# The order of the first loads in a gated linear attention and mixture-of-experts kernel

## The chip, the cores and the metric

One NeuronCore of a Trainium2 chip runs the whole program. The metric is device time in microseconds of one execution. The kernel before takes 376.09 us (median of three runs, 374.07 to 376.36).

## What is computed

The reference has two parts. The first is a gated linear attention: 4 batches, 8 heads, 768 positions, 48 channels a head. For every batch and head a 48 x 48 state is carried along the positions:

```
f = 1 / (1 + exp(-f_logit))
for t in range(S):
    state = f[:, :, t, :, None] * state + einsum('bhd,bhe->bhde', k[:, :, t], v[:, :, t])
    y[:, :, t] = einsum('bhd,bhde->bhe', q[:, :, t], state)
```

The second part takes the 3072 rows of 384 channels as tokens: `logits = x @ w_gate`, each token goes to its best of 8 experts, in order of arrival up to a capacity of 768, an expert is relu(x w1) w2 with 1024 hidden channels, and the row is scaled by its softmax weight.

## The kernel before

**Blocks and slots.** Attention runs over 24 blocks of 128 positions, six to a batch. The order of the work is written out by hand: `prologue()` brings the first blocks in, and `slot(n)` for n from 0 to 24 issues one stage of several blocks. In slot n, TensorE (PE) transposes k and q of block n+2 (`kq_in`), makes the scores of block n+1 (`scores_pe`), adds to block n what the state carries in (`inter`), updates the state (`update`), applies the masked scores of block n to v (`values`), and turns block n-1 into token rows with gate logits (`rows_pe`). Each engine runs its instructions in the order in which this code issues them, so an instruction that waits holds all that stands behind it on its engine.

**The other engines.** VectorE (DVE) makes the decays by scans (`decay`, `decay_back`) and scales the transposed k and q. ScalarE (ACT) takes the sigmoid of the gates of two blocks at a time (`sig`, tile pf) and copies PSUM out. GpSimd (POOL) copies k and q of a block into a padded tile (`kq_pad`, tile kqp), masks the scores (tile AT, L434), makes the carried state (`carry`, tile S, L508), and sends token rows to their expert's rows in DRAM by an indirect DMA (`scatter`, L326, tensor disp). The first of these scatters is issued in slot 7, one a slot after that.

**Loads.** SyncE (SP) issues nearly all loads. `load` fills the next of 3 tiles of gates (f, two blocks each), 3 of k and q (kq), or 6 of v. `late_constants` (L278) fetches the gate weights, four small transfers into the tile identc that `rows_pe` multiplies by; in the prologue they stand behind k, q of block 3 and v of block 1. `zero_disp` (L345) clears 256 rows of disp by one transfer of 402 KB from a tile of zeros: for expert 0 in the list of loads of slot 1, for the ninth group of rows in that of slot 3. A scatter writes the same tensor, so the first of them waits until the clears have landed.

**PE's fillers.** In the prologue `keep_busy` puts 7, 4 and 2 multiplications of the identity between the first steps. Transposing k and q of one block is one loop in which an instruction on partitions 0 to 63 (k) is followed by one on 64 to 127 (q).

Of the kernel before, what the change touches and what calls it, by code (L numbers as in the profile page):

```python
# [9 lines left out]
F32 = mybir.dt.float32  # L10
# [4 lines left out]
AF = mybir.ActivationFunctionType  # L15
# [5 lines left out]
P = 128  # L21
# [8 lines left out]
def kernel(  # L30
# [12 lines left out]
    nc = tc.nc  # L43
    B, H, S, D = q.shape
    N, DM = out.shape
    NE = w_gate.shape[1]
    DF = w1.shape[2]
    NP = H // 2
    HALF = 384
    C = 128  # L50
# [32 lines left out]
    psT = ctx.enter_context(tc.tile_pool(name="psT", bufs=2, space=PSUM))  # L83
# [96 lines left out]
    loads, pf, kqp = {}, [], []  # L180
    for nm in ("f", "kq", "v"):
        for i in range(NLOAD[nm]):
            if nm == "v":
                t = apool.tile([P, H, 64], F32, name=f"ld_{nm}{i}")
                nc.gpsimd.memset(t[:, :, D:], 0.0)
            else:
                t = apool.tile([P, H, 2, D], F32, name=f"ld_{nm}{i}")
            loads[nm, i] = t
    for made, nm, n in ((pf, "pf", 2), (kqp, "kqp", 2)):
        for i in range(n):  # L190
            t = apool.tile([P, 2, H, 64], F32, name=f"{nm}{i}")
# [3 lines left out]
    def pairs(nm, n, nt):  # L195
        b, t0 = n // CPB, n % CPB * C
        return srcs[nm][b, :, t0 : t0 + nt, :].rearrange("h (t j) d -> t h (j d)", j=2)

    def load(nm, n):
        if n >= (NT // 2 if nm == "f" else NT):  # L200
            return
        t = loads[nm, n % NLOAD[nm]]
        if nm == "v":
            b, t0 = n // CPB, n % CPB * C
            nc.sync.dma_start(t[:, :, :D], srcs[nm][b, :, t0 : t0 + C, :].rearrange("h p d -> p h d"))
            return
        t = t.rearrange("t h j d -> t h (j d)")
        if nm == "kq":
            for h, x in enumerate(nm):
                nc.sync.dma_start(t[64 * h : 64 * h + 64], pairs(x, n, C))  # L210
        elif n == 0:
            for h, queue in enumerate((nc.sync, nc.scalar)):
                hs = slice(4 * h, 4 * h + 4)
                queue.dma_start(t[:64, hs], pairs(nm, 0, C)[:, hs])
        else:
            nc.sync.dma_start(t, pairs(nm, 2 * n, 2 * C))

    def loaded(nm, n):
        return loads[nm, n % NLOAD[nm]]

    for nm, n in (("f", 0), ("kq", 0), ("kq", 1), ("f", 1), ("kq", 2), ("v", 0), ("f", 2)):
        load(nm, n)
        if (nm, n) == ("kq", 0):
            nc.sync.dma_start(loads["f", 0].rearrange("t h j d -> t h (j d)")[64:], pairs("f", 1, C))
# [5 lines left out]
    for i in range(2):  # L230
        t = apool.tile([P, NP * C], F32, name=f"Suf{i}")
# [5 lines left out]
    for i in range(2):  # L237
        t = apool.tile([P, NP, 64], F32, name=f"S{i}")
# [12 lines left out]
    identc = const.tile([P, NP, XW], F32, name="identc")  # L251
    put_off(nc.gpsimd.memset, identc, 0.0)
    for g in range(2):
        r = slice(64 * g, 64 * g + D)
        for b in range(2):
            h = g ^ b
# [21 lines left out]
    def late_constants():  # L278
        gates_of = w_gate.rearrange("(a b s d) e -> b s d a e", b=2, s=2, d=D)
        for g in range(2):  # L280
            for b in range(2):
                nc.sync.dma_start(identc[64 * g : 64 * g + D, b::2, 2 * D :], gates_of[b, g ^ b])
    ohc = const.tile([P, NE], BF16, name="ohc")
    lt = const.tile([P, NS, NS], F32, name="lt")
    put_off(nc.gpsimd.memset, lt, 1.0)
# [14 lines left out]
    for i in range(2):  # L300
        t = const.tile([P, NE], BF16, name=f"base{i}")
# [43 lines left out]
    def zero_disp(v):  # L345
        ins = nc.sync.dma_start(
            disp[v * RPE : v * RPE + 2 * P, :].rearrange("(a p) w -> p a w", p=P),
            zero.unsqueeze(1).broadcast_to([P, 2, W]),
        )
        after(ins, pace["ins"], "behind the first loads")  # L350

    def sig(u):
        if u >= NT // 2:
            return
        cuts = (0, 64, P) if u == 0 else (0, P)
        for r0, r1 in zip(cuts, cuts[1:]):
            pace["ins"] = nc.scalar.activation(
                pf[u % 2][r0:r1, :, :, :D], loaded("f", u)[r0:r1].rearrange("t h j d -> t j h d"), AF.Sigmoid
            ).ins

    def transposes(*dsts):
        for p in range(NP):
            for j in range(2):
                for t, src, h in dsts:
                    r = slice(64 * h, 64 * h + 64)
                    nc.tensor.transpose(  # L366
                        t[:R, p, j::2], src[r, j, 2 * p : 2 * p + 2].rearrange("t s d -> t (s d)")[:, :R], ident[r, r]
                    )
        return [t[:R].rearrange("r p t -> r (p t)") for t, src, h in dsts]
# [3 lines left out]
    def keep_busy(m):  # L373
        pw = psA.tile([P, P], F32, name="psA")
        for _ in range(m):
            nc.tensor.matmul(pw, ident, ident, start=True, stop=True)  # L376

    def f_in(*ns):
        made = [(psF.tile([P, NP, C], F32, name="psF"), pf[n // 2 % 2], n % 2) for n in ns]
        for n, F in zip(ns, transposes(*made)):  # L380
            Fs[n] = F
# [21 lines left out]
    def kq_pad(n):  # L403
        if n < NT:
            src = loaded("kq", n).rearrange("t h j d -> t j h d")
            if n - 3 < PAD_ACT:
                nc.gpsimd.tensor_copy(kqp[n % 2][:, :, :, :D], src)
            else:
                nc.scalar.activation(kqp[n % 2][:, :, :, :D], src, AF.Copy)

    def kq_in(n):
        pts = transposes(*((psT.tile([P, NP, C], F32, name="psT"), kqp[n % 2], h) for h in range(2)))
        for nm, pt, by, made in (("kT", pts[0], Sufb[n % 2], kTs), ("qT", pts[1], Rqs.pop(n), qTs)):
            t = abuf.tile([P, NP, C], F32, name=nm, bufs=3)
            nc.vector.tensor_tensor(t[:R].rearrange("r p t -> r (p t)"), pt, by[:R], op=ALU.mult)
            made[n] = t
# [120 lines left out]
    def rows_pe(n):  # L537
        yT = yTs.pop(n)
        px = psA.tile([P, NP, XW], F32, name="psA")
        for p in range(NP):  # L540
            for t in range(2):
                ts = slice(64 * t, 64 * t + 64)
                m_pe = nc.tensor.matmul(px[ts, p, :], yT[:R, p, ts], identc[:R, p, :], start=True, stop=True)  # L543
        marks[n] = [m_pe]
        return px
# [3 lines left out]
    def row_at(n):  # L549
        return ring[:, n % RING]  # L550
# [136 lines left out]
    def flush_scatter():  # L687
        if queue:
            n = queue.pop(0)
            late = n >= SPLIT  # L690
            ins = scatter(disp, ri_of.pop(n), row_at(n), NV * RPE - 1, ("disp", "late") if late else ("disp",))
            if not late:
                early_ins[:] = [ins]
# [76 lines left out]
    def prologue():  # L770
        keep_busy(7)
        nc.scalar.activation(warm, direv[:, :1], AF.Sigmoid)
        sig(0)
        f_in(0)
        decay_back(0, decay(0))
        kq_pad(0)
        load("kq", 3)
        load("v", 1)
        late_constants()
        keep_busy(4)  # L780
        kq_in(0)
        f_in(1)
        decay_back(1, decay(1))
        kq_pad(1)
        later_ops(put_off_ops)
        keep_busy(2)
        kq_in(1)
        sig(1)
        kq_pad(2)
        pas = scores_pe(0)  # L790
        f_in(2)
        decay_back(2, decay(2))
        scores_out(0, pas)
        pks = keys_pe(0)
        keys_out(0, pks)
        f_in(3)
        load("kq", 4)
        load("v", 2)
        load("kq", 5)
        load("f", 3)  # L800
    ends = {g + m - 1: (g, m) for g, m in GROUPS}

    def rank(g, pool):
# [8 lines left out]
    def loads_of(n):  # L812
        load("v", n + 3)
        if 0 < n < PAD_ACT:
            load("kq", n + 6)
        if n == 0:
            load("f", 4)
        if n == 2:
            nc.sync.dma_start(cap_i, capacity.bitcast(I32).partition_broadcast(P))
        if n in (1, 3):  # L820
            zero_disp(0 if n == 1 else NE)
        for k, at in enumerate(PIECE_LOAD):
            if at == n:
                pieces[k] = weight_piece(wsets[0], 0, raw0, k)

    def slot(n):
# [17 lines left out]
            choose_first(*half.pop())  # L844
        for g in full:
            choose_sum(*g)
        if n == 1:
            f_in(4)
        if kqn:
            kq_in(n + 2)  # L850
        if n % 2 and fn and n not in (1, 9, 15):
            f_in(n + 3, n + 4)
        if nxt:
            scores_out(n + 1, pas)
        if n == 0:
            sig(2)
        if prev and cur and first(n):
            y_out(n - 1)
# [31 lines left out]
        if nxt:  # L890
            for s in range(SCATTERS.get(n, 2)):
                flush_scatter()
        if fn:
            F = decay(n + 3)
        if prev:
            px = rows_pe(n - 1)
            if tail:
                rows_logits(n - 1, px)
                rows_copy(n - 1, px)
                chosen[n - 1] = choose_one(row_at(n - 1), abuf, tallies[-1][:, 1:2]), 1  # L900
            else:
                rows_copy(n - 1, px)
                rows_parts(n - 1, px)
# [15 lines left out]
        while full:  # L919
            g = full.pop()  # L920
            half.append((*g, choose_max(*g)))
        if prev and done and not tail:
            g, m = done
# [11 lines left out]
        if tail:  # L935
            early_job(n, 2)
            g, m = done
# [325 lines left out]
    xgs, made = {}, {}  # L1263
# [227 lines left out]
```

## Time and profile before

| what | before |
|---|---|
| median of three runs | 376.09 us |
| the profiled execution | 375.17 us, span 373.4 us, granted clock 0.99 |
| PE busy | 362.1 us, 97% of the span |
| DVE, ACT, POOL busy | 247.8, 223.8, 166.5 us |
| moved by DMA | 67.86 MB, mean 182 GB/s |

Attention fills the first 150 us or so of the span, the experts the rest. The page shows PE above nine tenths in nearly all of 40 slices, and the 16 DMA engines above nine tenths in the slices from 9 to 121 us.

### The profile page before, as it was taken

What the parts mean: (1) busy time and instruction counts of PE and PEld (TensorE: products, weight loads), DVE (VectorE), ACT (ScalarE), POOL (GpSimd) and SP (SyncE); (2) the same over time, 40 slices, a digit from 0 to 9 for tenths busy, and PEclk for the clock granted to TensorE, in tenths of its full rate; (3) what the DMA queues carried; (4) which work ended last, traced back from release to release, by engine and by line L of the source; (5) the groups of instructions that cost most, each with busy time, mean ns of one, the idle gap of its engine ahead of it and who ended that gap; (6) DMA issues with size and microseconds to landing.
All of it is one profiled execution on the core that took longest, in us unless ns stands there. A gap on an engine that the chain in (4) does not pass through costs nothing.

```text
span 373.4 us, 10082 instructions
## 1 busy us (share of the span) xinstructions
PE 362.1 (97%) x3895; PEld 340.8 (91%) x3895; DVE 247.8 (66%) x533; ACT 223.8 (60%) x458; POOL 166.5 (45%) x275
## 2 busy tenths in 40 slices
PE   8999999999899999999999999999999999999993
PEld 7999898888787889999899999999999999999993
DVE  4898988979687866753676296857757665570300
ACT  3356677877586763255477475759578586583310
POOL 6665556675757675235613702127117244144012
PEclk9999999999899999999999999999999999999997
DMA  8999999999997432476696979799797997721001
GB/s 153 187 177 224 205 207 227 256 214 226 213 227 164 130 114 105 133 237 204 191 239 188 286 196 242 212 187 319 169 204 247 172 208 253 129 94 52 14 23 40
DMA packets 111351, 67.86 MB, mean 182 GB/s; under 512 B 93646, under 2 KB 105844, under 8 KB 111296
## 3 DMA queue, kind: packets, MB, share of 16 engines
q1 hardware_dynamic: 107504, 57.09, 69.1%
q0 software_dynamic: 3520, 9.97, 7.7%
q8 instruction: 32, 0.52, 0.6%
q14 instruction: 23, 0.19, 0.2%
q10 hardware_dynamic: 272, 0.10, 0.1%
HBM read 49.46 MB, written 11.43 MB: 163 GB/s over the span
## 4 chain that ended last, share of the span: by engine, by line
PE 84%; issue 8%; ACT 3%; POOL 2%; DVE 1%; POOLq 1%; ACTq 0%
PE psM L1222 15%; PE psA L754 9%; PE psM L1015 9%; PE psT L754 9%; PE psM L754 7%; PE psA L426 6%; PE psY L522 6%; PE psA L543 5%; PE psT L366 4%; PE psY L468 3%; PE psA L488 3%; PE psT L451 3%; PE psF L366 2%; POOL out_dram L326 2%; PE psA L376 2%
## 5 line engine op out<-in xcount | busy, mean ns | idle before, releaser
L326 POOL DMA_INDIRECT out_dram<-yo,g_ti x30 | 31.3, 1042 | 55.6 <-ACT yo L1019 31.7
L434 POOL TENSOR_SCALAR_AFFINE_SELECT AT<-AT 128x512 f32<-128x512 f32 x48 | 29.4, 637 | 23.3 <-ACT AT L432 23.2
L1015 PE MATMUL psM<-w2h,hh 128*128 128x384 f32 (+2 forms) x112 | 37.5, 340 | 0.0
L1015 PE MATMUL psM<-w2l,hh 128*128 128x384 f32 (+2 forms) x112 | 37.3, 338 | 0.0
L1015 PE MATMUL psM<-w2h,hl 128*128 128x384 f32 (+2 forms) x112 | 37.2, 338 | 0.0
L135 ACT ACTIVATE w2h<-raw 128x768 fp32r<-128x768 f32 x32 | 27.0, 844 | 11.2 <-DMA raw<-in_moe_w_dram 11.2
L1222 PE MATMUL psM<-hh,w2h 128*128 128x440 f32 (+3 forms) x96 | 33.7, 351 | 0.0
L1222 PE MATMUL psM<-hh,w2l 128*128 128x440 f32 (+3 forms) x96 | 33.7, 351 | 0.0
L1222 PE MATMUL psM<-hl,w2h 128*128 128x440 f32 (+3 forms) x96 | 33.6, 350 | 0.0
L144 DVE TENSOR_TENSOR w2l<-raw,w2h 128x768 fp32r<-128x768 f32 x28 | 27.8, 994 | 7.7 <-ACT w2h L135 6.9
L386 DVE TENSOR_TENSOR_SCAN Suf<-psF,direv 112x511 f32<-112x511 f32 x24 | 29.1, 1212 | 4.5 <-PE psF L366 4.5
L432 ACT ACTIVATE AT<-psA 128x512 f32<-128x512 f32 x48 | 26.4, 612 | 8.9 <-PE psA L426 5.6
L1242 POOL COPY yo<-yq 128x384 uint16<-128x384 uint16 (+4 forms) x16 | 11.9, 790 | 40.1 <-DMA yq<-yp 38.2
L426 PE MATMUL psA<-qT,kT 48*128 48x128 f32 x384 | 29.4, 293 | 0.0
L400 DVE TENSOR_TENSOR_SCAN Rq<-psF,d 112x512 f32<-112x512 f32 x24 | 29.4, 1223 | 0.0
L326 POOL DMA_INDIRECT disp<-rows,ri x24 | 24.8, 1034 | 9.5 <-issue 4.3
L144 DVE TENSOR_TENSOR w1l<-raw,w1h 128x1024 fp32r<-128x1024 f32 x21 | 26.5, 1269 | 2.9 <-ACT w1h L135 2.6
L761 DVE SCALAR_TENSOR_TENSOR hl<-psA,hh 128x224 fp32r<-128x224 f32 (+8 forms) x26 | 14.2, 547 | 21.3 <-ACT hh L760 19.3
L559 ACT ACTIVATE rows<-psA 128x384 f32<-128x384 f32 x24 | 11.8, 491 | 26.0 <-PE psA L543 19.6
L522 PE MATMUL psY<-AT,ld_v 128*48 128x128 f32 (+1 forms) x384 | 26.9, 278 | 0.0
L426 PEld LDWEIGHTS psA<-qT,kT 48*128 48x128 f32 x384 | 25.8, 201 | 0.5 <-issue 0.5
L135 ACT ACTIVATE w1h<-raw 128x1024 fp32r<-128x1024 f32 x24 | 24.8, 1060 | 1.9 <-DMA raw<-in_moe_w_dram 1.9
(253 smaller groups left out, 1041.7 us busy)
## 6 DMA issues: line engine op xcount, KB each, us to landing
raw<-in_moe_w_dram SPq DMA_DIRECT2D x24, 512.0 KB
raw<-in_moe_w_dram SPq DMA_DIRECT2D x32, 384.0 KB
ld_kq<-in_k_dram SPq DMA_DIRECT2D x24, 192.0 KB
ld_kq<-in_q_dram SPq DMA_DIRECT2D x24, 192.0 KB
ld_v<-in_v_dram SPq DMA_DIRECT2D x24, 192.0 KB
ld_f<-in_f_logit_dram SPq DMA_DIRECT2D x11, 384.0 KB
xg<-disp SPq DMA_DIRECT2D x6, 589.5 KB
xg<-disp SPq DMA_DIRECT2D x3, 393.0 KB
```

Source lines behind the costliest of these rows:

```text
L135: return nc.scalar.activation(hi, raw, AF.Copy)
L144: engine.tensor_tensor(lo[cs], raw[cs], hi[cs].bitcast(F32), op=ALU.subtract)
L326: ins = nc.gpsimd.indirect_dma_start(out=dst, out_offset=bass.IndirectOffsetOnAxis(ap=idx, axis=0), in_=rows, in_offset=None, bounds_check ...
L386: nc.vector.tensor_tensor_scan(out=_view(Suf[:R], m - 1, [[-1, m]]), data0=_view(F, m, [[-1, m]]), data1=_view(direv[:R], m - 1, [[-1, m]] ...
L400: nc.vector.tensor_tensor_scan(out=Rq[:R], data0=F, data1=d1[:R], initial=0.0, op0=ALU.mult, op1=ALU.max)
L426: nc.tensor.matmul(pas[s][:, p], kTs[n][r, p], qTs[n][r, p], start=True, stop=True)
L432: nc.scalar.activation(AT[:, s], pas[s], AF.Copy)
L434: nc.gpsimd.affine_select(AT[:, s], AT[:, s], pattern=[[0, NP], [1, C]], compare_op=ALU.is_ge, fill=0.0, base=0, channel_multiplier=-1)
L522: nc.tensor.matmul(py[b][64 * g : 64 * g + m, a, :], vt[:, 2 * p + s, :m], AT[:, s, p, :], start=(first(n) and a == 0), stop=(a == NP // 2 ...
L754: nc.tensor.matmul(ph[:, :T], a[:, c, fs], x[:, c, :T], start=(n == 0), stop=(n == 3 * DT - 1))
L1015: nc.tensor.matmul(py[:n], x[:, ks], a[:, ft], start=(ft == 0 and m == 0), stop=(ft == FT - 1 and m == 2))
L1222: nc.tensor.matmul(pys[c][:, :T], a[:, ft, cs], x[:, :T], start=(ft == 0 and n == 0), stop=(ft == FT - 1 and n == 2))
```

## The change

Five edits, all in attention's first seven slots:

- The four transfers of the gate weights are issued by ACT instead of SP, at the same place of the code, behind the sigmoids of blocks 0 and 1.
- The gates of blocks 4 and 5 (f 2) are loaded behind k and q of block 3 instead of ahead of them, and those of blocks 6 and 7 (f 3) ahead of k and q of block 5 instead of behind.
- The clears of disp move from the lists of slots 1 and 3 to those of slots 4 and 6.
- Block 0 begins in halves: the first sigmoid is cut into heads 0 to 3 and 4 to 7, the padding copy into k and q, and the 16 transposes of k and q into 8 of k and then 8 of q.
- The sigmoid of blocks 4 and 5 moves from slot 0 to slot 1, and block 4's gates are transposed behind `rows_pe` of slot 1 instead of ahead of `kq_in`.

```diff
-    for nm, n in (("f", 0), ("kq", 0), ("kq", 1), ("f", 1), ("kq", 2), ("v", 0), ("f", 2)):
+    for nm, n in (("f", 0), ("kq", 0), ("kq", 1), ("f", 1), ("kq", 2), ("v", 0)):
...
-                nc.sync.dma_start(identc[64 * g : 64 * g + D, b::2, 2 * D :], gates_of[b, g ^ b])
+                nc.scalar.dma_start(identc[64 * g : 64 * g + D, b::2, 2 * D :], gates_of[b, g ^ b])
...
-        cuts = (0, 64, P) if u == 0 else (0, P)
-        for r0, r1 in zip(cuts, cuts[1:]):
+        cuts = ((0, 64, 0, H // 2), (0, 64, H // 2, H), (64, P, 0, H)) if u == 0 else ((0, P, 0, H),)
+        for r0, r1, h0, h1 in cuts:
...
-                nc.gpsimd.tensor_copy(kqp[n % 2][:, :, :, :D], src)
+                for r in (slice(0, 64), slice(64, P)) if n == 0 else (slice(0, P),):
+                    nc.gpsimd.tensor_copy(kqp[n % 2][r, :, :, :D], src[r])
...
-        pts = transposes(*((psT.tile([P, NP, C], F32, name="psT"), kqp[n % 2], h) for h in range(2)))
+        made = [(psT.tile([P, NP, C], F32, name="psT"), kqp[n % 2], h) for h in range(2)]
+        pts = transposes(*made) if n else [transposes(one)[0] for one in made]
...
         load("kq", 3)
+        load("f", 2)
         load("v", 1)
...
         load("v", 2)
+        load("f", 3)
         load("kq", 5)
-        load("f", 3)
...
-        if n in (1, 3):
-            zero_disp(0 if n == 1 else NE)
+        if n in (4, 6):
+            zero_disp(0 if n == 4 else NE)
...
-        if n == 1:
-            f_in(4)
...
-        if n == 0:
+        if n == 1:
             sig(2)
...
+        if n == 1:
+            px = rows_pe(0)
+            f_in(4)
         if fn:
             F = decay(n + 3)
         if prev:
-            px = rows_pe(n - 1)
+            px = px if n == 1 else rows_pe(n - 1)
```

**SP, slots 5 to 7.** Before, between the load of v of block 9 (tile ld_v_112) and that of block 10 (ld_v_114):

```order
L205 DMA ld_v_112<-in_v_dram 128x8x48
L210 DMA ld_kq_103<-in_k_dram 64x8x96
L210 DMA ld_kq_103<-in_q_dram 64x8x96
L216 DMA ld_f_101<-in_f_logit_dram 128x8x96
L205 DMA ld_v_114<-in_v_dram 128x8x48
```

With the change:

```order
L205 DMA ld_v_112<-in_v_dram 128x8x48
L210 DMA ld_kq_103<-in_k_dram 64x8x96
L210 DMA ld_kq_103<-in_q_dram 64x8x96
L346 DMA disp<-zero 128x2x393
L216 DMA ld_f_101<-in_f_logit_dram 128x8x96
L205 DMA ld_v_114<-in_v_dram 128x8x48
```

The second clear now stands behind k and q of block 12 and ahead of the gates of blocks 14 and 15; everything that SP issued ahead of those gates is still ahead, but for the four transfers of gate weights.

**POOL, slots 7 and 8.** The first scatter and what stands around it, with the semaphores that it waits for (DMAHW: a transfer's landing). Before:

```order
L508 TENSOR_TENSOR S_147<-U,pendall 112x4x48 [waits DVE_49]
L326 DMA disp<-rows,ri 32256x393 [waits DMAHW1_49]
L434 AFFINE_SELECT AT<-AT 128x512 [waits Activation_49] x2
L508 TENSOR_TENSOR S_149<-U,pendall 112x4x48 [waits DVE_49]
L326 DMA disp<-rows,ri 32256x393
```

With the change:

```order
L512 TENSOR_TENSOR S_146<-U,pendall 112x4x48 [waits DVE_49]
L326 DMA disp<-rows,ri 32256x393 [waits DMAHW4_49,DMAHW3_49]
L438 AFFINE_SELECT AT<-AT 128x512 [waits Activation_49] x2
L512 TENSOR_TENSOR S_148<-U,pendall 112x4x48 [waits DVE_49]
L326 DMA disp<-rows,ri 32256x393
```

The scatter's place is the same; the two semaphores that it waits for are those of the two clears. Behind it stand the mask of block 9's scores and the state that block 9 starts from.

**PE, prologue.** From the first transposes of gates to those of block 1. Before:

```order
L366 MATMUL psF<-ident,pf_118 112x64 [waits Activation_49,Pool_49]
L366 MATMUL psF<-ident,pf_118 112x64 x7
L376 MATMUL psA<-ident 128x128 x4
L366 MATMUL psT<-ident,kqp_122 112x64 [waits Pool_49]
L366 MATMUL psT<-ident,kqp_122 112x64 x15
L366 MATMUL psF<-ident,pf_118 112x64 [waits Activation_49]
```

With the change:

```order
L368 MATMUL psF<-ident,pf_118 112x64 [waits Activation_49,Pool_49]
L368 MATMUL psF<-ident,pf_118 112x64 x3
L368 MATMUL psF<-ident,pf_118 112x64 [waits Activation_49]
L368 MATMUL psF<-ident,pf_118 112x64 x3
L378 MATMUL psA<-ident 128x128 x4
L368 MATMUL psT<-ident,kqp_122 112x64 [waits Pool_49]
L368 MATMUL psT<-ident,kqp_122 112x64 x7
L368 MATMUL psT<-ident,kqp_122 112x64 [waits Pool_49]
L368 MATMUL psT<-ident,kqp_122 112x64 x7
L368 MATMUL psF<-ident,pf_118 112x64 [waits Activation_49]
```

Four transposes of gates no longer wait for the second half of the sigmoid, and the 16 of k and q, which alternated, are 8 of k followed by 8 of q.

## Rows read from the trace of the kernel before

**Rows 1.** The page: span, busy time of each engine, granted clock in 40 slices.
```profile
span 373.4 us, 10082 instructions
PE 362.1 (97%) x3895; PEld 340.8 (91%) x3895; DVE 247.8 (66%) x533; ACT 223.8 (60%) x458; POOL 166.5 (45%) x275
PEclk9999999999899999999999999999999999999997
```

**Rows 2.** PE's timeline, prologue and slot 1: start, length, instructions.
```profile
5.21 1.07 PE L366 MATMUL psF<-ident,pf 64*112 64x64 f32 x8
6.21 2.07 PE L376 MATMUL psA<-ident 128*128 128x128 f32 x8
8.21 1.10 PE L366 MATMUL psT<-ident,kqp 64*112 64x64 f32 x16
...
12.14 2.02 PE L426 MATMUL psA<-qT,kT 48*128 48x128 f32 x16
...
20.13 1.12 PE L426 MATMUL psA<-qT,kT 48*128 48x128 f32 x16
```

**Rows 3.** ACT's timeline: sigmoids of the gates; in brackets the idle time before.
```profile
4.22 0.84 ACT L357 ACTIVATE pf<-ld_f 64x768 f32<-64x768 f32 x1 [1.15 <-DMA ld_f<-in_f_logit_dram]
...
11.67 0.84 ACT L357 ACTIVATE pf<-ld_f 128x768 f32<-128x768 f32 x1 [2.90 <-DMA ld_f<-in_f_logit_dram]
...
28.25 0.84 ACT L357 ACTIVATE pf<-ld_f 128x768 f32<-128x768 f32 x1 [0.32 <-DMA ld_f<-in_f_logit_dram]
```

**Rows 4.** SP's timeline: start and length of a transfer's issue.
```profile
14.54 3.40 SPq L282 DMA_DIRECT2D identc<-in_moe_w_gate_dram  x4
...
18.69 0.63 SPq L210 DMA_DIRECT2D ld_kq<-in_q_dram  x1
...
21.46 0.57 SPq L216 DMA_DIRECT2D ld_f<-in_f_logit_dram  x1
...
28.08 0.63 SPq L210 DMA_DIRECT2D ld_kq<-in_q_dram  x1
...
41.85 0.79 SPq L346 DMA_DIRECT2D disp<-zero  x1
...
55.21 2.03 SPq L216 DMA_DIRECT2D ld_f<-in_f_logit_dram  x1
```

**Rows 5.** Stretches of 2 us: busy time of each engine, clock, DMA share, GB/s.
```profile
18.00:20.00 2.00, 2.00 (x47) 1.76 (x45) 1.58 (x4) 1.32 (x3) 1.22 (x2) 1.00 0.30 49
20.00:22.00 2.00, 2.00 (x48) 2.00 (x46) 1.97 (x4) 1.66 (x6) 1.27 (x2) 1.00 1.22 232
...
98.00:100.00 2.00, 1.27 (x30) 0.84 (x27) 1.29 (x2) 1.63 (x3) 1.92 (x5) 0.98 1.21 258
100.00:102.00 2.00, 2.00 (x32) 2.00 (x30) 1.25 (x2) 0.00 (x0) 0.90 (x3) 0.50 1.09 231
102.00:104.00 2.00, 2.00 (x25) 1.80 (x23) 1.93 (x6) 1.88 (x5) 1.12 (x2) 0.67 1.03 157
```

**Rows 6.** POOL's timeline: padding copies, then slots 7 and 8 from the first scatter.
```profile
7.12 0.82 POOL L407 COPY kqp<-ld_kq 128x768 f32<-128x768 f32 x1 [1.12 <-DMA ld_kq<-in_q_dram]
...
22.66 0.83 POOL L407 COPY kqp<-ld_kq 128x768 f32<-128x768 f32 x1 [1.33 <-DMA ld_kq<-in_q_dram]
...
33.70 0.83 POOL L407 COPY kqp<-ld_kq 128x768 f32<-128x768 f32 x1 [4.18 <-DMA ld_kq<-in_q_dram]
...
53.84 1.19 POOL L326 DMA_INDIRECT disp<-rows,ri  x1 [0.38 <-issue]
56.20 1.22 POOL L434 TENSOR_SCALAR_AFFINE_SELECT AT<-AT 128x512 f32<-128x512 f32 x2 [1.17 <-ACT AT L432]
57.56 0.51 POOL L508 TENSOR_TENSOR S<-U,pendall 112x192 f32<-112x192 f32 x1
```

**Rows 7.** PE's timeline, slot 9: what reads the carried state (L468).
```profile
59.77 0.86 PE L366 MATMUL psT<-ident,kqp 64*112 64x64 f32 x16
60.56 0.67 PE L468 MATMUL psY<-qT,S 48*64 48x128 f32 x16
```

More of the change, by code (lines that the diff above doesn't have):

```diff
@@ L354, in sig @@
             return
-        cuts = (0, 64, P) if u == 0 else (0, P)
-        for r0, r1 in zip(cuts, cuts[1:]):
+        cuts = ((0, 64, 0, H // 2), (0, 64, H // 2, H), (64, P, 0, H)) if u == 0 else ((0, P, 0, H),)
+        for r0, r1, h0, h1 in cuts:
             pace["ins"] = nc.scalar.activation(
-                pf[u % 2][r0:r1, :, :, :D], loaded("f", u)[r0:r1].rearrange("t h j d -> t j h d"), AF.Sigmoid
+                pf[u % 2][r0:r1, :, h0:h1, :D],
+                loaded("f", u)[r0:r1, h0:h1].rearrange("t h j d -> t j h d"),
+                AF.Sigmoid,
             ).ins
```

## The prediction, made before the changed kernel ran

> **What bounds the kernel now.** I began with the page. PE is busy 97% of the span, every other engine two thirds or less [rows 1], so a transfer or an engine counts only where PE waits for it. The changed code lies in the first 60 us. There PE's timeline hardly has a hole, and two things are to be seen in it. First, PE works at half speed until about 18 us: the 16 score multiplications of a block take 2.02 us at 12.14 and 1.12 us at 20.13 [rows 2]. The clock row reads full from the start [rows 1], so it does not show this first stretch; by the lengths of the rows it is the lower of the two levels (1.2 GHz), the later one the upper (2.4 GHz). Second, k's and q's transposes run side by side: 16 of them take 1.10 us, and the 8 of one block's gates, which all lie on the same partitions, take 1.07 [rows 2]. Then I read the loads. The transfers come a long time behind their issue: from SP's row to the end of the wait it is 4.0 us for one half of k and q (18.69 to 22.66), 5.6 for another (28.08 to 33.70) and 6.8 for the gates of two blocks (21.46 to 28.25) [rows 3, 4, 6]. The DMA engines are behind, and SP's place in its own list, not the need of a block, says when something lands.
>
> **First sigmoid in halves.** The sigmoid of 0.84 us starts at 4.22 when its data are there, and PE's first transposes start at 5.21, right behind it [rows 2, 3]. In halves, the first four transposes run while ACT makes the second half. That hides up to half of the 1.07 us; two short instructions cost more than a long one, so I take 0.4 us earlier, between 0 and 0.5.
>
> **k and q of block 0 apart.** The padding copy of 0.82 us begins at 7.12, when q has landed [rows 6]; k's own copy can go ahead of it, q's ends where it did. PE comes to these transposes at 8.21, straight from its fillers [rows 2], when q's copy has been done for a quarter of a microsecond. So there is no wait to save here; instead, 8 of k and then 8 of q lose the overlap. Twice the 1.07 us of the gates' row instead of 1.10 is 1.0 us more; part of each row is the tail of its last instruction, so I take 0.9, between 0 and 1.0. With the 0.4 gained before, PE is 0.5 us late at the lower level. When the clock has risen, the same work takes half the time, so 0.2 us is left in the end (from -0.5 to +1.0).
>
> **Gate weights on ACT.** Four issues took SP 3.40 us [rows 4]. On ACT they stand between the second half of block 0's and 1's sigmoid and that of blocks 2 and 3, which waited 2.90 us for its data until 11.67 [rows 3]; that idle time hides most of the 3.40. What sticks out, up to 0.5 us, is hidden too, since PE wants this tile only behind the scores that began at 12.14 and last to 14.2 [rows 2]. I cost it at nothing. If each issue took much longer, the sigmoid would be late for PE; that is a rival below.
>
> **Order of f 2, k and q of block 3, f 3, k and q of block 5.** The same bytes in another order, with no wait of PE on any of them in these slots: nothing. If the cover were gone, the loss would be that of one late block, as below.
>
> **Sigmoid of blocks 4 and 5, and block 4's transposes, later in slot 1.** The eight transposes stay eight. They now stand behind `rows_pe`, and DVE's scan for block 4 starts that much later, but its result is used only in slot 2. DVE is busy 66% of the span [rows 1], so it catches up: nothing. If the tile came late, PE would wait up to the 0.84 us of a sigmoid.
>
> **The clears in slots 4 and 6.** This is the term that decides. The second clear was issued at 41.85, and the first scatter, at 53.84, did not have to wait for it: 0.38 us of idle time, all of it "issue" [rows 4, 6]. The scatter keeps its place, and POOL executes in order. When does the clear land now? It stands where SP issued the gates of 55.21 [rows 4]. Ahead of it is one clear less, its own: 402 KB at 232 GB/s [rows 5], 1.7 us, so 53.5. The hole that the four gate issues made is gone as well: 49 GB/s in 18 to 20 us against 232 in the next two [rows 5] are 0.37 MB, 1.6 us of DMA work. The gate weights must still be moved, so not all of this is saved; I take 0.4 us and get 53.1, between 51.9 (all saved) and 55.2 (nothing saved, not even for the clear). From issue to landing I take the 6.8 us of the load that is nearest in size, the 393 KB of two blocks' gates, with 4.0 us as the lower bound. So the clear lands at 59.9, between 55.9 and 62.0. The Trainium skill says ("DMA: Bandwidth & Descriptors", section "Issuing engines are not separate DMA queues") that issuing from several engines saves only the issuing sequencer's time, which is usually small; the rows show that here it was a hole in the stream. By the rule alone nothing of the hole comes back, the clear lands at 60.3, and the sum is 0.4 us higher.
>
> What is queued behind the waiting scatter? Its own 1.19 us, two masks of block 9's scores (1.22 together) and the state for block 9 (0.51) [rows 6]: 2.9 us, with the hand-overs seen between these rows 3.1 us. PE reads that state at 60.56 in slot 9 [rows 7], at 60.8 with the 0.2 us from the prologue. In the kernel before it was ready at 58.07, so there were 2.5 us in hand. With the clear at 59.9 it is ready at 63.0, and PE waits 2.2 us (0 to 4.5). The masks are ready before `values` wants them, so this wait is not paid twice; the next scatters find the clear done.
>
> **Sum.** 0.2 + 2.2 = 2.4 us. PE gets nothing of it back, since it is the bound afterwards. On the profiled execution (375.17 us: a span of 373.4 and 1.8 around it) this makes 377.6. The median of the runs is 0.9 above that execution, and I predict on it: 378.5 us, 0.6% slower.
>
> **Rivals.**
> *The wait also costs clock.* In 98 to 100 us PE was busy only 1.27 of 2.00 us, and then the granted clock fell to 0.50 and stood at 0.67 in the stretch after [rows 5]. The lost shares (0.02, 0.50, 0.33 of 2 us each) make 1.7 us. A wait of 2.2 us is longer than the 0.7 missing there, which speaks for it; but the clock stays up through other short waits. It would give 380.2.
> *The clears land in time.* If the second one has landed by 57.7, POOL's 3.1 us fit before 60.8 and nothing waits. For it: 4.0 us have been seen from issue to landing, and without the first scatter's writes in between the stream is a little lighter. Against it: in these rows a load of that size took 6.8 us. Only the prologue would be left: 376.3, or, if PE overlaps q's transposes with what stands next to them so that only the 0.4 us of the first halves count, 375.7, faster than before. Everything hangs on the 57.7.
> *The gate weights hold ACT.* If they took 2 us each and not 0.85, the sigmoid of blocks 2 and 3 would start at about 17 us instead of 11.67, and PE, which wants it at 14.2, would wait some 3.5 us, at the lower level, with the scatter's wait then shorter by as much: about 379.5. Nothing but the unknown queue speaks for it. In this case the edit would do the opposite of what it says.
>
> **Numbers.** The forecast (378.5) gets 0.42, with the clock 0.28, in time 0.22, ACT held 0.05, others 0.03. The bounds of the wait alone spread the forecast over 376.3 to 380.8. The range 375.2 to 381.2 takes in the first two and most of the third. I count more than 1% as a difference that this measurement can tell, 372.3 and 379.9 here. Slower than that: most of the clock case and the upper end of the forecast, 0.29. Faster than that would need 3.8 us, and no term offers it: 0.04. Within 1%: 0.67.
>
> **What would show it.** Right: in POOL's timeline the first scatter sits behind an idle time of 5 us or more that a transfer ended, and L472 of slot 9 on PE has 1 to 4 us of idle time before it, ended by the state. The first transposes of k on PE last about 1 us and q's follow, so that block 1's gates come about 0.5 us later. The hole at 18 to 20 us in the DMA row is gone. Wrong: the scatter starts within 4 us of its old place and PE does not wait in slot 9, or PE's prologue ends earlier than before. Then the landing, 53.1 + 6.8, is the step that failed.

## The result and the profile after

| what | before | changed |
|---|---|---|
| median of the runs beside each other | 375.66 us (6 runs, 373.8 to 376.36) | 380.32 us (6 runs, 379.5 to 382.5) |
| ratio of the medians | | 1.0142, 95% interval 1.0104 to 1.018 |
| the profiled execution | 375.17 us, span 373.4 | 382.5 us, span 380.8 |

The changed kernel is 1.4% slower. 378.5 us was predicted, with a range of 375.2 to 381.2 and a chance of 0.29 for a loss of more than 1%. The profiled execution of the changed kernel is the slowest of its six; e8 below profiles the same kernel again, in a more usual one. I read the profile in the order in which the prediction asked for it: the page, POOL and PE around the first scatter, the clock, the prologue.

The page of the changed kernel: span, busy time of each engine, granted clock in 40 slices.

```profile
span 380.8 us, 10088 instructions
PE 365.6 (96%) x3895; PEld 343.6 (90%) x3895; DVE 248.0 (65%) x533; ACT 224.6 (59%) x459; POOL 168.3 (44%) x276
PEclk9999999699999999999999999999999999999999
```

Against [rows 1], PE has the same 3895 instructions and 3.5 us more of busy time, and the span is 7.4 us longer: part of the loss is idle time and part is work done at a lower clock. The clock row has a 6 in its eighth slice (67 to 76 us), where before had its 8 in the eleventh.

POOL's timeline of the changed kernel at the first scatter; the columns are start, length, instruction, and in brackets the idle time before it.

```profile
63.74 1.19 POOL L326 DMA_INDIRECT disp<-rows,ri  x1 [7.58 <-DMA disp<-zero]
64.96 1.22 POOL L438 TENSOR_SCALAR_AFFINE_SELECT AT<-AT 128x512 f32<-128x512 f32 x2
66.15 0.50 POOL L512 TENSOR_TENSOR S<-U,pendall 112x192 f32<-112x192 f32 x1
```

The scatter that waited 0.38 us for its issue in [rows 6] now waits 7.58 us for a clear. The two masks and the state for block 9 stand behind it. PE's timeline in slot 9 shows who pays (L472 is the line that was L468 before):

```profile
62.97 0.62 PE L368 MATMUL psT<-ident,kqp 64*112 64x64 f32 x16
66.70 1.13 PE L472 MATMUL psY<-qT,S 48*64 48x128 f32 x16 [3.11 <-POOL S L512]
```

In [rows 7] the same pair runs with no gap, and the second row takes 0.67 us. Now it starts 3.11 us after PE was free, and takes 1.13 us. The chain of waits of the changed kernel, from 30 to 70 us, goes the same way (start, length, step):

```profile
55.88 6.93 DMA disp<-zero
...
62.85 0.76 issue
...
66.18 0.48 POOL S L512
66.66 0.04 issue
66.70 1.13 PE psY L472 x15
```

Ahead of the first of these lines the chain is almost nothing but PE from 49 us on. Then it is one transfer, 6.93 us from issue to landing, and the POOL rows shown above (in part left out here), of which the state is the last. The landing at 62.81 (55.88 + 6.93) does not start the scatter at once: another 0.93 us goes by until 63.74.

The changed kernel in stretches of 2 us (busy time of PE, PEld, DVE, ACT and POOL, granted clock, DMA share, GB/s):

```profile
18.00:20.00 2.00, 2.00 (x36) 1.87 (x34) 1.12 (x3) 1.01 (x2) 1.23 (x2) 1.00 1.05 160
...
64.00:66.00 2.00, 0.00 (x0) 0.00 (x0) 0.91 (x2) 1.35 (x2) 1.98 (x3) 0.99 0.96 189
66.00:68.00 2.00, 1.30 (x20) 0.97 (x22) 0.00 (x0) 0.00 (x0) 1.81 (x4) 0.50 1.25 249
68.00:70.00 2.00, 2.00 (x37) 1.87 (x37) 0.00 (x0) 0.00 (x0) 1.63 (x4) 0.50 1.12 304
70.00:72.00 2.00, 2.00 (x26) 2.00 (x24) 1.96 (x5) 0.65 (x3) 1.34 (x2) 0.50 1.20 221
72.00:74.00 2.00, 2.00 (x31) 1.71 (x29) 1.80 (x6) 1.21 (x4) 0.19 (x1) 0.81 1.24 271
...
100.00:102.00 2.00, 2.00 (x58) 1.57 (x56) 1.29 (x2) 0.96 (x2) 1.23 (x2) 1.00 1.11 224
```

PE does nothing from 64 to 66 us, and then works at the lower level (0.50 of full speed, 1.2 GHz) until about 72.8 us, by the 0.81 of the stretch from 72 to 74. The fall that before had at 100 us [rows 5] is not there. The hole at 18 to 20 us is gone, 160 GB/s instead of 49.

The prologue on PE, then on ACT, in the changed kernel:

```profile
1.84 3.36 PE L378 MATMUL psA<-ident 128*128 128x128 f32 x14 [1.84 <-POOL ident masks.py:199]
5.12 1.10 PE L368 MATMUL psF<-ident,pf 64*112 64x64 f32 x8
...
8.16 1.57 PE L368 MATMUL psT<-ident,kqp 64*112 64x64 f32 x16
...
19.92 1.86 PE L526 MATMUL psY<-AT,ld_v 128*64 128x128 f32 x15
22.01 1.12 PE L430 MATMUL psA<-qT,kT 48*128 48x128 f32 x16
```

```profile
8.01 2.34 ACTq L282 DMA_DIRECT2D identc<-in_moe_w_gate_dram  x4
11.77 0.85 ACT L357 ACTIVATE pf<-ld_f 128x768 f32<-128x768 f32 x1 [2.98 <-DMA ld_f<-in_f_logit_dram]
```

The first transposes start 0.09 us earlier than in [rows 2]; the 16 of k and q take 1.57 us instead of 1.10. ACT's sigmoid of blocks 2 and 3 starts 0.10 us later than in [rows 3]. In this execution PE still worked at the lower level at 20 us (1.86 us for 15 instructions), where before was already at the upper one at 20.13; with the 0.4 us of the prologue that puts slot 1's scores 1.9 us later. The late rise is not the change's doing: in e8, the same kernel, those scores start at 19.13.

SP's timeline of the changed kernel, at the places of [rows 4]:

```profile
28.11 0.63 SPq L210 DMA_DIRECT2D ld_kq<-in_q_dram  x1
...
38.89 0.38 SPq L216 DMA_DIRECT2D ld_f<-in_f_logit_dram  x1
...
55.88 2.58 SPq L346 DMA_DIRECT2D disp<-zero  x1
```

And two rows of SP's timeline of the kernel before, the first clear and the next gates:

```profile
32.10 0.79 SPq L346 DMA_DIRECT2D disp<-zero  x1
...
38.08 0.43 SPq L216 DMA_DIRECT2D ld_f<-in_f_logit_dram  x1
```

The q half issued at 28.08 before is issued at 28.11 now, with the same loads ahead of it. In this execution SP was ahead in between (k of block 4 went out at 15.80, before at 18.04) and had lost it again by then. The gates that went out at 38.08 behind a clear go out at 38.89 now, with no clear ahead of them. One pair of executions is little to go by; the profiles of the experiments are added to it further down.

### The profile page after: what moved, and what is told of

Its sections match the earlier page's. It is cut to its first block, busy times and chain, and to the rows that moved or that the text cites. A ratio compares the mean times of both kernels' runs of the same rounds, so it can differ in the third digit from the quotient of the medians.

```text
span 380.8 us, 10088 instructions
## 1 busy us (share of the span) xinstructions
PE 365.6 (96%) x3895; PEld 343.6 (90%) x3895; DVE 248.0 (65%) x533; ACT 224.6 (59%) x459; POOL 168.3 (44%) x276
## 4 chain that ended last, share of the span: by engine, by line
PE 77%; issue 10%; DMA 4%; POOL 4%; ACT 3%; DVE 1%; POOLq 1%; ACTq 0%; SPq 0%; DVEq 0%
PE psM L1228 14%; PE psA L758 9%; PE psT L758 8%; PE psM L1021 7%; PE psA L430 6%; PE psM L758 5%; PE psY L526 5%; PE psA L547 5%; PE psT L368 3%; PE psY L472 3%; PE psA L492 3%; PE psF L368 3%; PE psT L455 2%; DMA disp<-zero 2%; POOL out_dram L326 2%
## 5 line engine op out<-in xcount | busy, mean ns | idle before, releaser
L526 PE MATMUL psY<-AT,ld_v 128*48 128x128 f32 (+1 forms) x384 | 27.8, 285 | 0.0
```

The costliest lines, as they stand in the source:

```text
L526: nc.tensor.matmul(py[b][64 * g : 64 * g + m, a, :], vt[:, 2 * p + s, :m], AT[:, s, p, :], start=(first(n) and a == 0), stop=(a == NP // 2 ...
```

## The experiments

The theory: the late second clear holds POOL's first scatter, what stands behind it makes PE wait in slot 9, and the clock falls in this wait. The rivals: the prologue (k and q apart, order of loads) costs the time; or the later loads do, wherever the clears stand. The kernels of one group (e1 to e4, e5 to e8, e9 and e10) ran on one chip, the groups on different ones, each beside new runs of the kernel before, whose median is given. Lines with - are those of the changed kernel where nothing else is said.

### e1 and e2: the clears alone, from both sides

e1 is the changed kernel with the clears back in their old lists:

```diff
-        if n in (4, 6):
-            zero_disp(0 if n == 4 else NE)
+        if n in (1, 3):
+            zero_disp(0 if n == 1 else NE)
```

> The changed kernel with one edit undone: the clears of disp stand in the lists of slots 1 and 3 again. Theory (the second clear lands too late, the first scatter holds POOL, POOL holds PE in slot 9, and PE's clock then falls): the scatter starts at its old place, near 56 us, PE has no wait in slot 9 and no fall of the clock behind it; 375.5 to 376.8 us, 0 to 0.3% above the kernel before, the rest being k and q of block 0 apart. Rival (the prologue and the order of loads cost most, the wait is made up later): 378.5 us or more. Rival 2 (the earlier loads are worth something that the wait hides): below 375 us.

e2 is the kernel before with that edit made the other way round, and nothing else of the change.

> The kernel before with one edit done: the clears in the lists of slots 4 and 6. Theory: POOL's first scatter waits for the landing 5 us or more, PE waits 2 to 4 us in slot 9, the clock may fall for 3.4 us or twice that; 378.5 to 381 us, most of the 4.7 us of the whole change. Rival (the prologue and the order of loads cost most): 375 to 377 us.

Before ran at 373.5 us. e1: 373.15 us, ratio 0.9976 (0.9935 to 1.0017). e2: 377.39 us, ratio 1.0118 (1.0067 to 1.0168). The times expected above were reckoned from the 375.66 us of the first result; on this chip the kernel before is 2 us faster, so the ratios decide. By them the loss comes and goes with the place of the clears, and the other four edits together show no effect clear of the noise, neither a cost nor the gain of the second rival. POOL's first scatter and PE in slot 9, in e1 and then in e2:

```profile
56.80 1.19 POOL L326 DMA_INDIRECT disp<-rows,ri  x1 [0.38 <-issue]
...
63.52 0.67 PE L472 MATMUL psY<-qT,S 48*64 48x128 f32 x16
```

```profile
63.81 1.19 POOL L326 DMA_INDIRECT disp<-rows,ri  x1 [9.82 <-DMA disp<-zero]
...
66.76 1.13 PE L468 MATMUL psY<-qT,S 48*64 48x128 f32 x16 [5.84 <-POOL S L508]
```

e2's PE came earlier than that of the changed kernel's first profile and waited longer, 5.84 us, for a state that was there at the same moment: the end of the wait is set by the clear, not by PE.

### e3: the clears half-way

```diff
-        if n in (4, 6):
-            zero_disp(0 if n == 4 else NE)
+        if n in (3, 5):
+            zero_disp(0 if n == 3 else NE)
```

> The changed kernel with the clears in the lists of slots 3 and 5, one slot earlier than in the change. Theory with its point of decision (POOL has about 2.5 us in hand, only what goes beyond holds PE): the second clear lands near 59 us, the scatter waits 2 to 3 us for it, the state for block 9 is ready before PE asks for it at about 63, no wait of PE in slot 9; 375.5 to 377 us, as with the clears in slots 1 and 3. Rival (every wait of the scatter costs its length): 378 to 379 us. Rival (the prologue costs most): 378.5 or more.

374.09 us against 373.5, ratio 1.0009 (0.9966 to 1.0051). The scatter does wait, PE does not, and the profile's mean granted clock is 0.996. POOL's and PE's rows of e3:

```profile
56.96 1.19 POOL L326 DMA_INDIRECT disp<-rows,ri  x1 [2.83 <-DMA disp<-zero]
...
60.99 0.67 PE L472 MATMUL psY<-qT,S 48*64 48x128 f32 x16
```

2.83 us of waiting on POOL cost nothing. The cost is not in proportion to the scatter's delay; it begins where the state behind the scatter is late for PE.

### e4 and e6: k and q of block 0 alternating again

```diff
-        pts = transposes(*made) if n else [transposes(one)[0] for one in made]
+        pts = transposes(*made)
```

> The changed kernel with block 0's transposes of k and q in one loop again, alternating. Theory: 16 of them take 1.1 us instead of 1.57 and all that follows in the prologue stands 0.4 to 0.5 us earlier at the lower clock; the wait in slot 9 stays and grows by what PE gains, so the time stays within 0.5 us of the changed kernel: 379.5 to 380.6 us. Rival (the 0.5 us decide when the clock rises, and so 1.7 us): 378 to 379 us.

e4: 376.51 us against 373.5, ratio 1.0076 (1.0029 to 1.0122). The wait in slot 9 is there (5.33 us). The time lies below both expected ranges, which were again reckoned from the first result. The changed kernel did not run in that group, so what the alternation gives back can't be read from it; the ratio lies within the interval of e8 below.

e6 adds e1's edit to this one.

> The changed kernel with two edits undone: the clears in slots 1 and 3, block 0's transposes of k and q in one loop. Theory: no wait in slot 9, and a prologue that is 0.4 to 0.5 us shorter at the lower clock than with the transposes apart: 0 to 0.6% faster than the kernel before. Rival (what is left of the change, the order of loads and ACT's issues, costs): slower than the kernel before.

374.48 us against 374.01, ratio 1.0016 (0.9979 to 1.0054). The expected gain did not show. Its profile has another wait, early in slot 1, which e1 has as well (1.33 us). PE's timeline of e6:

```profile
21.72 0.95 PE L492 MATMUL psA<-ld_v,kn 128*64 128x48 f32 x15 [1.37 <-DMA ld_v<-in_v_dram]
```

With the gates of blocks 4 and 5 ahead of it, v of block 1 can be late for PE when the prologue runs fast. In both profiles the granted clock is at 0.50 or 0.51 from 22 to 28 us, behind this wait.

### e8, e5 and e7: the same kernel again, the wait filled, the wait avoided

e8 is the changed kernel, unaltered, as the measure for e5 and e7.

> The changed kernel itself, on the chip of the next three, so that they can be compared with it. All theories: 1.0% to 1.8% slower than the kernel before; POOL's first scatter waits 7 to 10 us for the clear, PE 3 to 6 us in slot 9, the granted clock falls behind that wait.

Before ran at 374.01 us, e8 at 376.67, ratio 1.0077 (1.0042 to 1.0112). It is slower again, but by less than expected. e8's first scatter on POOL and L472 on PE, and then two of its stretches of 2 us:

```profile
62.36 1.19 POOL L326 DMA_INDIRECT disp<-rows,ri  x1 [9.17 <-DMA disp<-zero]
...
65.32 1.13 PE L472 MATMUL psY<-qT,S 48*64 48x128 f32 x16 [5.20 <-POOL S L512]
```

```profile
64.00:66.00 2.00, 0.68 (x14) 0.69 (x16) 0.00 (x0) 0.00 (x0) 1.83 (x4) 0.50 1.27 249
66.00:68.00 2.00, 2.00 (x39) 1.54 (x32) 0.00 (x0) 0.00 (x0) 1.89 (x5) 0.50 1.03 345
```

e5 lets PE multiply the identity while it waits:

```diff
         early_job(n, 0)
+        if n == 9:
+            keep_busy(10)
         if cur:
             inter(n)
```

> The changed kernel with ten multiplications of the identity (20 passes, 2.1 us at the upper clock) on PE in slot 9, between the transposes of k and q and the step that waits for POOL; their result is not used. They fill most of the wait and are over before it ends. Theory (part of the loss is the clock that falls because PE stood still): the wait for POOL ends where it did, but the clock does not fall behind it or for one stretch of 3.4 us less; 1.5 to 3.5 us below the changed kernel. Rival (the clock falls for another reason, or its fall is not paid): as the changed kernel, or up to 1 us slower.

374.5 us, ratio 1.0019 (0.9989 to 1.0049), and 2.2 us below e8 (376.67 - 374.5; the two intervals hardly overlap). The scatter starts when it does in e8 (62.30 against 62.36), but the clock does not fall. POOL's and PE's rows of e5, and one of its stretches of 2 us:

```profile
62.30 1.19 POOL L326 DMA_INDIRECT disp<-rows,ri  x1 [6.62 <-DMA disp<-zero]
...
63.07 2.50 PE L378 MATMUL psA<-ident 128*128 128x128 f32 x20 [0.38 <-ACT AT L436]
65.50 0.67 PE L472 MATMUL psY<-qT,S 48*64 48x128 f32 x16
```

```profile
66.00:68.00 2.00, 2.00 (x59) 1.84 (x53) 0.53 (x2) 0.00 (x0) 1.90 (x5) 1.00 1.07 304
```

PE begins L472 at 65.50 us, no earlier than in e8, so the fillers take nothing off the wait itself. What they take off is the work at half speed behind it: PE gets 59 instructions done from 66 to 68 us, in e8 39. One caution: in this execution PE came to slot 9 2.6 us later than in e8, so the pause that the fillers fill was some 2.6 us and not 5.2. The other executions have no profile, but their mean granted clock points the same way, 0.993 in the median against 0.985 in e8.

e7 leaves the clears late and moves the scatters instead: none in slots 7 and 8, two in 9 and 10.

```diff
-    SCATTERS = {n: 2 if n in (18, 19) else 0 if n == 20 else 1 for n in range(NT - 3)}
+    SCATTERS = {n: 2 if n in (9, 10, 18, 19) else 0 if n in (7, 8, 20) else 1 for n in range(NT - 3)}
```

> The changed kernel with the clears where the change put them (slots 4 and 6), but no scatter in slots 7 and 8 and two each in slots 9 and 10, so that the first one stands two slots further back in POOL's queue, behind the masks and the states of blocks 9 and 10. Theory (what costs is only what stands behind the waiting scatter): no wait of PE in slot 9, no fall of the clock there, within 0.4% of the kernel before. Rival (the clears' transfer in these slots costs by what it does to the loads): still 1% or more slower.

373.49 us against 374.01, ratio 0.9997 (0.9961 to 1.0034). The first scatter is as late as in e8, but PE has gone through slot 9 without a wait before it, as POOL's row of the scatter and PE's of slot 9 in e7 show:

```profile
62.85 1.19 POOL L326 DMA_INDIRECT disp<-rows,ri  x1 [0.43 <-issue]
...
59.49 0.67 PE L472 MATMUL psY<-qT,S 48*64 48x128 f32 x16
```

So neither the late clear nor the late scatter costs time. What costs is that the state for block 9 stands behind a waiting scatter.

### e9 and e10: a version meant to be faster, and the kernel before once more

e9 keeps the change, alternates k and q again as in e4, moves the clears to slots 2 and 4, and loads v of block 1 ahead of the gates of blocks 4 and 5:

```diff
         load("kq", 3)
-        load("f", 2)
         load("v", 1)
+        load("f", 2)
...
-        if n in (4, 6):
-            zero_disp(0 if n == 4 else NE)
+        if n in (2, 4):
+            zero_disp(0 if n == 2 else NE)
```

> The changed kernel with the clears in slots 2 and 4, block 0's k and q transposed in one loop, and v of block 1 loaded ahead of the gates of blocks 4 and 5. Theory: in two of the experiments with an early rise of the clock PE waited 1.3 us for that v in slot 1 and the clock fell behind it for 6.8 us; with the v some 2 us earlier PE doesn't wait for it there, nor for POOL in slot 9: 0.3% to 1.2% faster than the kernel before. Rival (the fall of the clock at 22 us has another cause, or PE waits for the gates of block 4 in its place): within 0.3% of the kernel before.

373.54 us against 372.63, ratio 1.0037 (0.9996 to 1.0078): no gain. The wait for v is gone, and in its place the gates of blocks 4 and 5 are late (1.12 us). PE's timeline of e9:

```profile
22.82 0.66 PE L368 MATMUL psF<-ident,pf 64*112 64x64 f32 x8 [1.12 <-ACT pf L357]
```

e10 is the kernel before, profiled again to see where it spends what e8 and e2 lose in slot 9 and partly get back later.

> The kernel before itself, for its profile on the chip of the other experiments. All theories: 0.995 to 1.005 of the runs of the kernel before; the profile of one execution shows at which slot the changed kernel's wait is made up again, if it is. Theory (PE is the bound throughout): slots 10 to 23 take the same time in both, to about 1 us, falls of the clock apart. Rival (after a wait the other engines are ahead, and later short waits of PE shrink): the kernel before loses 2 us or more in waits in slots 10 to 23 that the changed kernel doesn't have.

373.98 us against 372.63, ratio 1.002 (0.9977 to 1.0062). PE's timeline of e10 and then that of e8, at the first two transposes of token rows (tile xg), with e10's slot 9 ahead:

```profile
60.57 0.67 PE L468 MATMUL psY<-qT,S 48*64 48x128 f32 x16
...
125.42 0.69 PE L718 MATMUL psF<-ident,xg 128*128 128x128 f32 x2 [3.82 <-DMA xg<-disp]
130.19 0.66 PE L718 MATMUL psF<-ident,xg 128*128 128x128 f32 x4
```

```profile
128.66 0.44 PE L722 MATMUL psF<-ident,xg 128*128 128x128 f32 x2
131.23 0.66 PE L722 MATMUL psF<-ident,xg 128*128 128x128 f32 x4
```

In slot 9 e8 is 4.75 us behind e10 (65.32 against 60.57) and has a stretch at the lower clock still before it; at the second of the xg rows it is 1.04 us behind. In between, e10 waited 3.82 us for the first token rows to come back from DRAM, and e8, coming later, did not wait. The clock of e10 fell in this wait as well, so that some 2 us of work at half speed come on top. A stretch of 2 us of e10 behind the wait:

```profile
126.00:128.00 2.00, 2.00 (x32) 1.96 (x33) 0.78 (x2) 0.38 (x1) 0.30 (x1) 0.50 0.02 6
```

In this execution the rival came out: the kernel before loses more than 2 us here that the changed one does not. e3, e7 and e9, which reach this place early (by 122.4 us), wait there too, but less (0.92, 0.86 and 0.89 us). e4 comes late and still waits 0.39 us, and the first profile of the kernel before, which comes at 127.2, does not wait.

## Why the prediction was right, and where it was not

**Right: the place and the chain.** Each step of the clears' term is in the trace: the scatter behind an idle time that a transfer ended, masks and state behind it, L472 waiting 3.11 us, inside the 1 to 4 us that would show it. e1 and e2 show that this term decides and no other one to a degree that these runs can tell, e7 that it is the order on POOL, e3 that POOL has time in hand: 2.83 us of waiting pass unseen. The time itself was met with some luck. It lies inside the range, but 1.8 us above the forecast. It lies next to the 380.2 of the rival with the clock, but both terms of that rival, the wait and the fall, were too small, and not all that was lost there reached the median.

**Too small: the issue of the second clear.** The latency, 6.8 us, was right (6.93). The issue was not: 53.1 was predicted, and it came at 55.88, past my upper bound of 55.2. This is the latest of five profiles with that order. SP's timelines give, in us, when it issues q of block 6, and when it reaches the place of the second clear in the changed kernel (the issue of that clear, or of the gates of blocks 14 and 15 where it stands further up):

| order of the other loads | clears ahead of the place | profiles | q of block 6 | the place |
|---|---|---|---|---|
| as before | two | before, e10 | 28.08, 29.39 | 55.21, 56.05 |
| as before | one | e2 | 28.76 | 55.73 |
| as changed | two | e1, e3, e6, e9 | 27.67, 27.68, 27.39, 27.74 | 54.41, 55.31, 54.95, 54.65 |
| as changed | one | changed, e4, e5, e7, e8 | 28.11, 27.46, 27.83, 28.00, 27.32 | 55.88, 55.37, 54.60, 53.68, 54.43 |

The term that failed is the 1.7 us for the clear that no longer stands ahead. With the changed order the place is reached at 54.83 us on average behind two clears and at 54.79 behind one, so the clear taken away gave nothing. Its 402 KB at 232 GB/s were not time that the other loads could use. The stretch from 30 to 40 us, of before and of the changed kernel, shows the same in its last two columns:

```profile
30.00:40.00 10.00, 10.00 (x231) 9.18 (x232) 8.76 (x18) 6.55 (x19) 5.12 (x9) 1.00 1.04 200
```

```profile
30.00:40.00 10.00, 9.81 (x224) 8.85 (x222) 8.15 (x15) 5.86 (x18) 4.99 (x10) 1.00 1.02 148
```

The DMA engines are as busy without the clear as with it (1.02 and 1.04), and move a quarter less. The five profiles with a clear in this stretch show 198 to 202 GB/s, the seven without one 147 to 190.

The 0.4 us for the hole fared better. The changed order reaches the place some 0.8 us earlier than the old one (55.66 on average over its three profiles); which of the four other edits gives this was not tested, and single executions of one kernel differ by more. The Trainium skill's rule ("DMA: Bandwidth & Descriptors", section "Issuing engines are not separate DMA queues"), that issuing from several engines saves only the issuing time, would by the prediction's reading have brought nothing of the hole back and made the sum 0.4 us higher, still short. The first pair of profiles agrees (28.11 against 28.08); the whole table rather speaks against it, as far as single executions can tell.

**Too small: the hand-over.** I let POOL start with the landing. It started 0.93 us after it, and 0.93 to 0.94 us in e2, e4 and e8.

**The wait.** By these figures the state comes at 66.66 us, not 63.0. In the first profile PE's own lateness (3.0 us by the end of block 9's transposes, 63.59 against 60.56, of which 1.9 were there by slot 1's scores, 22.01 against 20.13) hid half of what its wait would have been. So it is luck that the 3.11 us lie inside my 1 to 4: in e8 and e2, where PE came on time, the wait was 5.20 and 5.84 us against the 2.2 predicted and its upper bound of 4.5.

**The wrong case: the clock.** I gave the fall of the clock 0.28 and forecast without it. It fell in every profile that had the wait and no fillers (the changed kernel, e2, e4, e8), and not in e5. It fell behind e10's wait of 3.82 us too. I had also priced it too low, 1.7 us, by a fall behind a gap of 0.7 us [rows 5]. Here PE worked at half speed from 66.70 to about 72.8 us, which is some 3 us of work; e5 against e8 measures 2.2 us in the end. With the first profile's wait of 3.1 us and this fall, 6 us would be lost, and the medians show 4.7 (380.32 - 375.66).

**Wrong in part: "PE gets nothing of it back".** In the first profile before has its own fall of the clock at 100 us [rows 5], which the changed kernel has not. In the later groups e10's wait for xg shows another way: a kernel that is early at slot 21 waits there, one that is late hardly or not. That fits e8's loss of 0.8% where slot 9 alone cost more. It is one execution of each kernel, and on different chips, so the share of it in the medians is not settled.

**The prologue.** The transposes apart cost 0.47 us (1.57 against 1.10) where I took 0.9; the Trainium skill's rule that weights are loaded under running multiplications only if those use other rows of the array ("TensorE: Matmul & The Clock Gate", section "The mechanism") speaks for the same sign, and the rows agree with it: k then q take longer than k and q in turn. The halves gave 0.09 us where I took 0.4, since PE was busy with its fillers until then (14 from 1.84 us on, 3.36 us long), not waiting for the sigmoid, as I had read it. Before, too, the fillers ended at 5.18 us, behind the sigmoid (5.06). The sum, 0.42 us late at the lower level (0.47, less the 0.05 by which the row starts earlier), is near the 0.5 predicted. The gate weights on ACT cost nothing, as predicted: 2.34 us of issue inside an idle time of 2.98. That they could hold ACT is refuted.

**The other edits.** "Nothing" holds for the order of f 2 and f 3 within the interval of e1. But there is a price that I did not see: v of block 1, now behind the gates of blocks 4 and 5, was late by 1.3 us in e1 and e6, and e9 shows that with v first the gates are late by 1.1 us. The loads there have no slack for either.

**Left open.** Why the changed kernel's first profile falls behind between 28 and 39 us, where the eight other profiles with its order of loads issue the same gates at 36.42 to 37.82 and not at 38.89; whether the alternation of k and q gains anything at the end (e4 and e6 can't tell); and why the loss is 1.4% in the first result and 0.8% in e8 (1.0104 to 1.018 against 1.0042 to 1.0112).

## What to carry to other kernels

A transfer that only has to be done by some time has its deadline not where its reader stands, but at the first instruction behind that reader, on the same engine, that a busy engine needs; here 2.83 us of waiting were free, and 7.6 to 9.8 us cost 0.8 to 1.4%. A transfer that moves down a saturated list need not bring forward what stood behind it: here 402 KB less ahead gained nothing, and a saving like this belongs in a sum only where a trace shows it. And where a change puts a wait of several us on TensorE, the work at the lower clock behind it belongs in the sum from the start; fillers in the wait take that part away.

## What the runs showed of the hardware

- After a pause of 3 us PE ran at the lower level for several us although it was busy again: from 66 to 72 us the changed kernel shows 0.50 in each stretch, PE busy 2.00 of 2.00 us in two of the three. With 20 multiplications of the identity in the pause it stayed at 1.00 (e5).
- An indirect DMA on POOL that waited for a transfer began 0.93 us after the landing (62.81 to 63.74), and 0.93 to 0.94 us in e2, e4 and e8.
- A stretch of 10 us of loads with a write of 402 KB among them moved 198 to 202 GB/s in five profiles, without it 147 to 190 in seven, at DMA shares of 1.04 to 1.12 and 0.84 to 1.11. SP reached a place further down its list at 54.83 us on average behind two such writes and at 54.79 behind one.
- Four issues of the gate weights took SP 3.40 us [rows 4] and ACT 2.34 us.
